# Four VectorE instructions of each weight conversion, spread over a step, in conversions that start two steps earlier

## The chip, the core and the metric

The kernel runs on one core of a Trainium2 chip. The metric is device time in microseconds (us): three runs of the kernel before gave a median of 691.45 us (688.99 to 691.76). Five engines work side by side, each through its own instructions in order: PE multiplies matrices and transposes, ACT applies functions and copies, DVE and POOL compute elementwise, and SP issues nearly all transfers from and to DRAM. Semaphores make an instruction wait for one of another engine; everything behind a waiting instruction on the same engine waits too.

## The reference

Three layers follow each other. All are computed in float32; the last layer's weights arrive as float64.

```
q_pool = mean of pairs of queries                        # 2 x 8 heads, 576 pooled queries, 1152 keys
attn   = softmax(q_pool @ k^T / 8) @ v                   # -> x: 1152 tokens x 512
e      = argmax over 8 experts of cosine(x, emb) / tau   # top-1 routing, gate = its softmax weight
y      = gate * (relu(x @ w1[e]) @ w2[e])                # w1: 512 x 1024, w2: 1024 x 512
out    = ((y @ w_a) * (y @ w_b)) @ w_out                 # w_a, w_b: 512 x 1536, w_out: 1536 x 512
```

## The kernel before

Every float32 operand is split into a rounded high part and the remainder (names ending in h or hi, and l or lo), and each product is three matmuls: high by high, high by low, low by high. ACT makes high parts, DVE or POOL subtracts to make low parts.

The program has three stages. The attention stage runs over 72 units of 128 queries. The experts' stage runs over steps m = 0 to 34; the numbers of steps below are these. The final layer runs over passes n = 1 to 37. The order of instructions on each engine is written out by hand: what stands where in the functions is what each engine gets.

The experts' stage has 32 pieces of work, one per step: a chunk of 256 of the 1024 hidden columns of one slot of tokens. Slots of two tiles (256 tokens) and of one tile (128 tokens) alternate by `ORDER`. `moe_step(m)` works on several pieces at once:

- `s1(m)` is PE's product of tokens and w1 (L890 for two tiles, 24 matmuls; L895 for one tile, 12 matmuls). `h_ev(m - 1)` takes its result one step later: for two tiles ACT makes hh (L902) and DVE hl (L903). For one tile ACT makes hs (L908), PE transposes it in `h_tr` (L915), and `h_ev2(m - 2)` one more step later makes hh on ACT and hl on DVE.
- `s2(m - 2)` is PE's product with w2 (L933; 12 matmuls for two tiles, 6 for one).
- `split1(m + 1)` makes w1h (ACT) and w1l (DVE) for the next step. `split2(m - 1)` and `split2b(m - 1)` make w2h (ACT or DVE) and two halves of w2l (POOL or DVE).
- `x_tr` and `x_ev` transpose and split the tokens of a slot: PE (L838), ACT (xhi), DVE (xlo). `y_ev` copies a finished slot out (ACT ys, L942). `load1` and `load2` issue the weights' loads on SP.

So PE's row in a step is s1(m), the transposes of hs of step m - 1, s2(m - 2), then transposes of tokens. hs(22), for example, is what PE needs between s1(23) and s2(21).

Beside that, from step 17 on, `advance` drives the conversions of the last layer's float64 weights, once at the end of every step. Each conversion covers 128 x 1024 weights; six run in the experts' stage (called conversions 1 to 6 here: w_a, w_b and w_out for the first 256 hidden columns, then the same for the next), and twelve in the final layer. `convert` is a generator; each `yield` ends its part of a step:

```
SP    raw <- DRAM          1 MB, issued in the step of W_AT; then CONV_LAG = 3 steps pass
ACT   cvt <- raw           L1075, scaled magnitude of the upper words (called Abs here)
DVE   cvt, four times      L1077, L1078, L1079, L1081 (called C1 to C4 here)
ACT   wh <- cvt            L71, high part (called W here)
POOL  wl <- cvt, wh        L75, low part in two halves
```

In the kernel before, Abs stands at the end of the third step after the load, C1 to C4 at the end of the fourth, W and the first half of wl at the end of the fifth. Loads start in steps 19, 21, 24, 27, 28, 31, so C1 to C4 stand at the ends of steps 23, 25, 28, 31, 32 and after the first elementwise work of the final layer. The tiles raw and cvt have two buffers each. In the final layer `f1` (L1165) multiplies by w_a and w_b, `f_ab` makes the product (asb, L1175; abh; abl), and `f2` (L1187) multiplies by w_out. The first products f1(0) stand in step 32, f1(1) in pass 1.

Of the kernel before, what the change touches and what calls it, by code (L numbers as in the profile page):

```python
# [14 lines left out]
U32 = mybir.dt.uint32  # L15
AF = mybir.ActivationFunctionType
ALU = mybir.AluOpType
# [26 lines left out]
LO_PARTS = range(48, 63)  # L44
ROUND1, P2_AT, DS = 3, 4, (1, 2, 1, 2, 1)
CONV_LAG, Y_LAG = 3, 4
W_AT = (19, 21, 24, 27, 28, 31)
W_AT2 = range(3, 27, 2)
W2_ACT = (1, 2, 3, 4, 5, 6, 7, 8, 9, 10, 12, 13, 16, 17, 18, 19, 21, 22, 24, 25, 27, 28, 31)
Y_AT, YB_AT = 20, 34  # L50
# [11 lines left out]
def fused(ctx, tc, q, k, v, emb, tau, w1, w2, wa, wb, wo, out):  # L62
    nc = tc.nc
# [386 lines left out]
    def pv(j, ps=None):  # L450

        pr, u = units[j]
        eT = U[j]["eT"]
        if place(j) == 0:
            G[j]["bank"] = (ps or ps_o)()
        cols = slice(0, 129) if u == 4 else slice(0, 65) if u < 4 else slice(64, 129)
        o = G[j]["bank"][:, 65 * place(j):65 * place(j) + cols.stop - cols.start]
        vh, vl = (preps[pr][x][:, :, cols] for x in ("vh", "vl"))
        for n in range(9):
            for x, v_ in ((0, vh), (0, vl), (1, vh)):  # L460
                nc.tensor.matmul(o, eT[:, 9 * x + n, :], v_[:, KEYS[n], :], start=(n == 0 and x == 0 and v_ is vh),  # L461
                                 stop=(n == 8 and x == 1))

    def xout(j):

        if not last(j):
            return
        pr, u = units[j]
        b, hp = divmod(pr, 4)
        p, w, n = G[j]["bank"], preps[pr]["ivsc"], place(j) + 1  # L470
        pg = p[:, :65 * n].rearrange("p (g d) -> p g d", g=n)
        rr = small.tile([P, 2], F32, name="r", bufs=3)
        nc.vector.tensor_scalar(out=rr[:, :n].unsqueeze(2), in0=pg[:, :, 64 * (u < 5):64 * (u < 5) + 1], scalar1=1e-9,
                                scalar2=None, op0=ALU.add)
        nc.vector.reciprocal(out=rr[:, :n], in_=rr[:, :n])
        stt = nc.vector.scalar_tensor_tensor
        if u == 4:
            for h in range(2):
                s, d = slice(64 * h, 64 * h + 64), slice(128 * hp + 64 * h, 128 * hp + 64 * h + 64)
                stt(out=xs[b][4][0:64, d], in0=p[s, 65 * h:65 * h + 64], scalar=w[s],  # L480
                    in1=rr[s, 0:1].to_broadcast([64, 64]), op0=ALU.mult, op1=ALU.mult)
        else:
            h, i = (0, u - 1) if u < 4 else (1, u - 6)
            stt(out=xt_[b][:, i:i + 2, 128 * hp + 64 * h:128 * hp + 64 * h + 64], in0=pg[:, :, h:h + 64], scalar=w,
                in1=rr.unsqueeze(2).to_broadcast([P, 2, 64]), op0=ALU.mult, op1=ALU.mult)
        G[j].clear()
        U[j].clear()
# [270 lines left out]
    def turn(kinds, columns=None):  # L758

        if cur[0] is None and queue:  # L760
            cur[:] = queue.popleft(), None
            cur[1] = next(cur[0])
        if cur[0] is not None and cur[1] in kinds:
            spare[0] = columns() if columns else None
            cur[1] = next(cur[0], None)
            if cur[1] is None:
                cur[0] = None
# [48 lines left out]
    NM = len(steps)  # L816
# [3 lines left out]
    def tiles(k):  # L820

        return 2 if k[1] < 2 else 1
# [12 lines left out]
    def x_tr(k, t, ps=None):  # L835
        pt = X[k]["pt"] = (ps or ps_t)()
        for c in range(4):
            nc.tensor.transpose(pt[:, P * c:P * c + P], X[k]["raw"][t][:, P * c:P * c + P], ident)  # L838

    def x_ev(k, t):  # L840
        pv_ = X[k].pop("pt").rearrange("p (c t) -> p c t", c=4)
        hi = X[k]["hi"][:, :, P * t:P * t + P]
        copy_hi(hi, pv_)
        sub_lo(X[k]["lo"][:, :, P * t:P * t + P], pv_, hi)
# [92 lines left out]
    def y_ev(k):  # L937
        b, s = k
        row = X[k]["row"] - (SMALL0 - 2 * NBIG * P if s >= 2 else 0)
        for t, y in enumerate(X[k].pop("y")):  # L940
            ys = moe.tile([P, DM], F32, name="ys")
            nc.scalar.activation(out=ys, in_=y, func=AF.Copy)  # L942
            nc.sync.dma_start(out=ybuf[b][row + P * t:row + P * t + P, :], in_=ys)
# [4 lines left out]
    def mt(f, m):  # L948
        if 0 <= m < NM:
            f(m)  # L950

    next_ = [1 + max(n for x in EARLY.values() for f, n in x if f == i) for i in (1, 2)]

    def moe_step(m):
        def turns(n, p=True):
            for _ in range(DS[n]):
                turn("de")
            turn("s")
            if p:
                turn("p", lambda: (ps_s().rearrange("p (j t) -> p j t", j=4), ps_s()))  # L960

        for k in X:
            if m == X[k]["l"] + 3:
                y_ev(k)
        for j in PVS.get(m - 1, ()):
            xout(j)
        turns(0, False)
        for k in X:
            if "pt" in X[k]:
                x_ev(k, X[k].pop("t"))  # L970
        mt(h_ev2, m - 2)
        mt(h_ev, m - 1)
        mt(s1, m)
        for n, j in enumerate(PVS.get(m, ())):
            pv(j, ps_m if units[j][1] == 4 else ps_o)
        turns(1)
        mt(h_tr, m - 1)
        mt(split1, m + 1)
        turns(2, False)
        mt(split2, m - 1)  # L980
        turns(3, False)
        mt(split2b, m - 1)
        mt(s2, m - 2)
        turns(4, m >= P2_AT)
        for k in X:
            t = m - X[k]["f"] + 1 + tiles(k)
            if 0 <= t < tiles(k):
                x_tr(k, t)
                X[k]["t"] = t
            if t == -1 and "raw" not in X[k]:  # L990
                x_load(k)
        la = LA[min(m, len(LA) - 1)]
        for f, x in ((load1, 0), (load2, 1)):
            while next_[x] < NM and next_[x] <= m + la[x]:
                f(next_[x])
                next_[x] += 1
# [61 lines left out]
    def convert(kind, c, dst, pool):  # L1058

        r = pool.tile([P, 1024, 2], U32, name="raw", bufs=2)  # L1060
        if kind < 2:
            src = (wa, wb)[kind].rearrange("(k p) f -> p k f", p=P)[:, :, 512 * c:512 * c + 512]
            nc.sync.dma_start(out=r.rearrange("p (k f) x -> p k (f x)", k=4), in_=src)
            sh, kw = "p (k f) -> p k f", dict(k=4)
        else:
            src = wo.rearrange("(j p) d -> p j d", p=P)[:, 2 * c:2 * c + 2, :]
            nc.sync.dma_start(out=r.rearrange("p (j d) x -> p j (d x)", j=2), in_=src)
            sh, kw = "p (j d) -> p j d", dict(j=2)
        for _ in range(CONV_LAG):
            yield  # L1070
        lo, hi = r[:, :, 0], r[:, :, 1]

        t = pool.tile([P, 1024], U32, name="cvt", bufs=2)
        tf = t.bitcast(F32)
        nc.scalar.activation(out=tf, in_=hi.bitcast(F32), func=AF.Abs, scale=2.0 ** -112)  # L1075
        yield
        nc.vector.tensor_scalar(out=tf, in0=tf, scalar1=CHI, scalar2=None, op0=ALU.min)  # L1077
        nc.vector.tensor_scalar(out=t, in0=t, scalar1=3, scalar2=1, op0=ALU.logical_shift_left, op1=ALU.bitwise_or)  # L1078
        nc.vector.scalar_tensor_tensor(out=t, in0=lo, scalar=29, in1=t, op0=ALU.logical_shift_right,  # L1079
                                       op1=ALU.bitwise_or)  # L1080
        nc.vector.scalar_tensor_tensor(out=t if dst is None else dst.bitcast(U32), in0=hi if dst is None else hi.rearrange(sh, **kw),  # L1081
                                       scalar=0x80000000, in1=t if dst is None else t.rearrange(sh, **kw),
                                       op0=ALU.bitwise_and, op1=ALU.bitwise_or)
        yield tf.rearrange(sh, **kw)

    wparts = {}
# [1 line left out]
    def weights(c, kind):  # L1088

        for f in convert(kind, c, None, wp):  # L1090
            yield
        sh = [P, 4, 256] if kind < 2 else [P, 2, DM]
        hi, lo = wparts[c, kind] = [wp.tile(sh, F32R, name=f"w{x}{kind}", bufs=2) for x in "hl"]
        copy_hi(hi, f)
        n = sh[1] // 2
        sub_lo(lo[:, :n], f[:, :n], hi[:, :n], nc.gpsimd)
        yield
        sub_lo(lo[:, n:], f[:, n:], hi[:, n:], nc.gpsimd)

    m = WP_AT  # L1100
# [104 lines left out]
    while m < NM + 3:  # L1205
# [7 lines left out]
        if m >= Y_AT:  # L1213
            drive()
        advance(m in W_AT)
        m += 1
# [37 lines left out]
    with tc.If(nc.values_load(ovf, min_val=0, max_val=2) > 0):  # L1254
        with tc.tile_pool(name="gen", bufs=1) as gen:
# [3 lines left out]
            for c in range(NC):  # L1259
                for kind in range(3):  # L1260
                    dst = wv[kind][:, :, 256 * c:256 * c + 256] if kind < 2 else wov[:, 2 * c:2 * c + 2, :]
# [5 lines left out]
            with tc.For_i(0, NE, 1) as e:  # L1267
# [8 lines left out]
                for b in range(NB):  # L1276
                    for i in range(5):
# [14 lines left out]
                        for j in range(8):  # L1292
                            nc.tensor.matmul(p, hT[:, P * j:P * j + P], w2t[:, j, :], start=j == 0, stop=j == 7)
                        nc.vector.scalar_tensor_tensor(out=yac[b][i], in0=p, scalar=gt[:, b, i:i + 1], in1=yac[b][i],
                                                       op0=ALU.mult, op1=ALU.add)
            for b in range(NB):
                for i in range(5):
# [21 lines left out]
                    m = P if i < 4 else 64  # L1319
# [5 lines left out]
CHI = 122879.9921875 * 2.0 ** -112  # L1325
# [32 lines left out]
```

## Time and profile before

| | |
|---|---|
| median of 3 runs | 691.45 us |
| the profiled execution | 693.38 us |
| its span, first to last instruction | 691.7 us |
| PE busy | 618.1 us (89%) |
| DVE busy | 493.5 us (71%) |
| ACT busy | 373.6 us (54%) |
| POOL busy | 322.3 us (47%) |
| mean granted PE clock | 0.948 of full speed |

The busy times are sums over stages of different kinds; where PE is idle is read from stretches of the span and from the waits of single instructions. An instruction of the timeline that stood idle carries in brackets for how long, and which instruction ended the wait. The experts' stage of interest (steps 22 to 34) runs from about 389 us to 462 us of the span; the final layer follows.

### The profile page before, as it was taken

To read this page: it belongs to the slowest core of one execution; us is meant where nothing else is said; L and a number is where in the kernel's file an instruction comes from. 1 tells how busy PE (TensorE), PEld (TensorE's weight loads), DVE (VectorE), ACT (ScalarE), POOL (GpSimd) and SP (SyncE) were. 2 spreads that over 40 slices of the span, in tenths; PEclk is the share of its full clock that TensorE was granted. 3 is DMA by queue.
4 is the path that set the end of the run, shared out by engine and by line. 5 is a ranking of instruction groups with operands and counts; after the bars stand their busy time and mean duration, and the time that the engine had idled before them with its cause. 6 is when DMAs were issued, how large, how long until landed. Compare 5 with 4: busy or idle time off the path is not lost.

```text
span 691.7 us, 13314 instructions
## 1 busy us (share of the span) xinstructions
PE 618.1 (89%) x5280; PEld 556.1 (80%) x5280; DVE 493.5 (71%) x796; ACT 373.6 (54%) x518; POOL 322.3 (47%) x271
## 2 busy tenths in 40 slices
PE   6688979889878788998989987969999999999996
PEld 5477767778767677998879877859999999999995
DVE  5978989887899977659947697974355575665523
ACT  3868886987665766456545675426243324233210
POOL 3958878785767941433424665673011212112100
PEclk9779999998988899999999998999999999999998
DMA  9979899998987789884898986454012213121012
GB/s 290 269 176 233 200 217 234 213 211 198 196 198 184 180 202 263 279 277 124 292 332 252 366 315 226 124 160 160 1 62 81 101 62 123 61 70 54 0 46 95
DMA packets 203075, 123.27 MB, mean 178 GB/s; under 512 B 149240, under 2 KB 174840, under 8 KB 203008
## 3 DMA queue, kind: packets, MB, share of 16 engines
q1 hardware_dynamic: 201536, 117.65, 62.3%
q0 software_dynamic: 1472, 4.72, 1.9%
q8 instruction: 43, 0.70, 0.4%
q14 instruction: 24, 0.20, 0.1%
HBM read 72.11 MB, written 13.67 MB: 124 GB/s over the span
## 4 chain that ended last, share of the span: by engine, by line
PE 49%; DVE 22%; ACT 4%; DMA 4%; issue 4%; POOL 1%; SPq 1%; DVEq 0%; ACTq 0%
PE ps_s L1165 21%; PE ps_s L890 4%; DVE nm L379 4%; PE ps_o L1187 4%; PE ps_m L1187 3%; PE ps_y L1187 3%; PE ps_o L461 2%; PE ps_s L374 2%; DVE vl L262 2%; DMA w2r<-in_moe_w_dram 2%; PE ps_m L933 2%; DMA eT<-ehl 2%; PE ps_y L933 1%; DVE cvt L1078 1%; DVE cvt L1079 1%
## 5 line engine op out<-in xcount | busy, mean ns | idle before, releaser
L407 POOL TENSOR_TENSOR ehl<-e,ehl 128x288 f16<-128x288 f32 (+1 forms) x99 | 152.3, 1557 | 63.7 <-issue 31.7
L75 POOL TENSOR_TENSOR wl<-cvt,wh 128x512 fp32r<-128x512 f32 x36 | 48.6, 1364 | 150.1 <-ACT wh L71 146.5
L75 POOL TENSOR_TENSOR w2l<-w2r,w2h 128x512 fp32r<-128x512 f32 x42 | 66.1, 1592 | 92.4 <-ACT w2h L71 46.9
L384 ACT ACTIVATE e<-ps_s,nm 128x1152 f32<-128x1152 f32 x72 | 87.8, 1220 | 37.2 <-DVE nm L379 25.1
L379 DVE TENSOR_REDUCE nm<-ps_s 128x1 f32<-128x1152 f32 x72 | 97.2, 1350 | 12.9 <-PE ps_s L374 12.7
L374 PE MATMUL ps_s<-kTh,qT 64*128 64x512 f32 (+2 forms) x480 | 98.2, 398 | 2.3 <-issue 1.2
L461 PEld LDWEIGHTS <-eT 128*128 128x128 f16 x1863 | 74.8, 102 | 16.6 <-issue 5.6
L461 PE MATMUL ps_o<-vh,eT 128*128 128x65 f16 (+1 forms) x1224 | 78.4, 203 | 10.3 <-DMA eT<-ehl 3.1
L374 PEld LDWEIGHTS ps_s<-kTh,qT 64*128 64x128 f32 x480 | 74.2, 206 | 8.5 <-issue 2.4
L461 PE MATMUL ps_o<-vl,eT 128*128 128x65 f16 (+1 forms) x612 | 73.2, 203 | 0.0
L1175 DVE TENSOR_TENSOR asb<-ps_s,asb 128x384 f32<-128x384 f32 x36 | 20.0, 554 | 69.1 <-PE ps_s L1165 69.1
L396 ACT ACTIVATE ehl<-e 128x1152 f16<-128x1152 f32 (+1 forms) x62 | 69.1, 1114 | 0.0
L71 ACT ACTIVATE abh<-asb 128x384 fp32r<-128x384 f32 x36 | 18.9, 525 | 84.3 <-DVE asb L1175 84.3
L374 PE MATMUL ps_s<-kTl,qT 64*128 64x512 f32 (+2 forms) x240 | 47.9, 367 | 1.5 <-DVE kTl L75 1.5
L1170 ACT ACTIVATE asb<-ps_s 128x384 f32<-128x384 f32 x36 | 17.7, 492 | 57.5 <-PE ps_s L1165 57.2
L374 PEld LDWEIGHTS ps_s<-kTl,qT 64*128 64x128 f32 x240 | 44.3, 209 | 2.1 <-DVE kTl L75 2.1
L75 DVE TENSOR_TENSOR w1l<-w1r,w1h 128x1024 fp32r<-128x1024 f32 x32 | 41.0, 1280 | 4.4 <-ACT w1h L71 3.6
L890 PE MATMUL ps_s<-xhi,w1l 128*128 128x256 f32 x128 | 38.0, 297 | 4.0 <-DVE w1l L75 4.0
L890 PE MATMUL ps_s<-xhi,w1h 128*128 128x256 f32 x128 | 38.4, 300 | 0.0
L75 DVE TENSOR_TENSOR abl<-asb,abh 128x384 fp32r<-128x384 f32 x36 | 20.7, 574 | 24.5 <-ACT abh L71 24.5
L890 PE MATMUL ps_s<-xlo,w1h 128*128 128x256 f32 x128 | 37.7, 294 | 0.0
L71 ACT ACTIVATE w1h<-w1r 128x1024 fp32r<-128x1024 f32 x32 | 34.0, 1063 | 0.0
(277 smaller groups left out, 1743.5 us busy)
## 6 DMA issues: line engine op xcount, KB each, us to landing
w1r<-in_moe_w_dram SPq DMA_DIRECT2D x32, 512.0 KB, 5.6
w2r<-in_moe_w_dram SPq DMA_DIRECT2D x32, 512.0 KB, 5.9
raw<-in_moe_w_a_dram SPq DMA_DIRECT2D x6, 1024.0 KB, 5.4
raw<-in_moe_w_b_dram SPq DMA_DIRECT2D x6, 1024.0 KB, 6.2
raw<-in_moe_w_out_dram SPq DMA_DIRECT2D x6, 1024.0 KB, 5.1
vs<-in_v_dram SPq DMA_DIRECT2D x8, 576.0 KB, 5.1
qs<-in_q_dram SPq DMA_DIRECT2D x16, 256.0 KB, 4.2
ks<-in_k_dram SPq DMA_DIRECT2D x7, 576.0 KB, 5.9
```

Of the source, the lines that this page charges most:

```text
L71: nc.scalar.activation(out=dst, in_=src, func=AF.Copy)
L75: (engine or nc.vector).tensor_tensor(out=dst, in0=src, in1=hi.bitcast(F32), op=ALU.subtract)
L374: nc.tensor.matmul(ps[:, c:c + n], qT[x][r:r + 64, o:o + 128], kT[y][r:r + 64, h, k0:k0 + n], start=i == 0, stop=i == len(ops) - 1)
L379: nc.vector.tensor_reduce(out=nm, in_=U[j]["ps"][:, 256:1408], axis=AX.X, op=ALU.max, negate=True)
L384: nc.scalar.activation(out=e, in_=U[j]["ps"][:, 256:1408], func=AF.Exp, bias=U[j]["nm"])
L396: nc.scalar.activation(out=ehl[:, 0, :c], in_=U[j]["e"][:, :c], func=AF.Copy)
L407: eng.tensor_tensor(out=ehl[:, 1, a:a + n], in0=U[j]["e"][:, a:a + n], in1=ehl[:, 0, a:a + n], op=ALU.subtract)
L461: nc.tensor.matmul(o, eT[:, 9 * x + n, :], v_[:, KEYS[n], :], start=(n == 0 and x == 0 and v_ is vh), stop=(n == 8 and x == 1))
L890: nc.tensor.matmul(p[:, 256 * j:256 * j + 256], a[:, kk, P * j:P * j + P], x[:, kk, :], start=(kk == 0 and x is xhi and a is w1h), stop=(k ...
L933: nc.tensor.matmul(y, a[:, j, P * t:P * t + P], w[:, j, :], start=(c == 0 and j == 0 and a is hh and w is w2h), stop=(c == 3 and j == 1 an ...
L1165: nc.tensor.matmul(p[:, :384], w[:, kk, :], y[:, kk, :], start=(kk == 0 and x == 0), stop=(kk == 3 and x == 2))
L1187: nc.tensor.matmul(F[n]["o"][t], a[:, P * t:P * t + P], w, start=(j == 0 and x == 0), stop=(j == 1 and x == 2))
```

## The change

The four DVE instructions of conversions 1 to 6 are no longer issued together. They go into a queue (`pieces`), and `moe_step` takes one from it at each of four places: ahead of s1, behind split1, behind split2 and behind split2b. A fifth entry marks the conversion as done. W_AT starts the loads earlier: steps 17, 19, 22, 24, 27, 29 in place of 19, 21, 24, 27, 28, 31, which is two steps for most, three for the fourth and one for the fifth. C1 to C4 of the six now stand in steps 22, 24, 27, 29, 32 and 34, one step later after their own load than before; W stands, as before, at the end of the fifth step after the load, which is now the step of C1 to C4 itself. The conversions of the final layer are as before.

```diff
-W_AT = (19, 21, 24, 27, 28, 31)
+W_AT = (17, 19, 22, 24, 27, 29)
...
+    pieces = deque()
+
+    def piece(n=1):
+        for _ in range(n):
+            if pieces:
+                pieces.popleft()()
+        if len(pieces) % 5 == 1:
+            pieces.popleft()()
+
     def moe_step(m):
...
         mt(h_ev, m - 1)
+        piece()
         mt(s1, m)
...
         mt(split1, m + 1)
+        piece()
         turns(2, False)
         mt(split2, m - 1)
+        piece()
         turns(3, False)
         mt(split2b, m - 1)
+        piece()
         mt(s2, m - 2)
...
         nc.scalar.activation(out=tf, in_=hi.bitcast(F32), func=AF.Abs, scale=2.0 ** -112)
         yield
-        nc.vector.tensor_scalar(out=tf, in0=tf, scalar1=CHI, scalar2=None, op0=ALU.min)
...
+        ops = (
+            lambda: nc.vector.tensor_scalar(out=tf, in0=tf, scalar1=CHI, scalar2=None, op0=ALU.min),
...
+            lambda: done.append(True))
+        if dst is None and m < NM + 3:
+            pieces.extend(ops)
+            while not done:
+                yield
+        else:
+            for f in ops:
+                f()
         yield tf.rearrange(sh, **kw)
...
         for f in convert(kind, c, None, wp):
-            yield
+            if f is None or m >= NM + 3:
+                yield
```

DVE's row around steps 22 and 23, before: xlo, hl(20), hl(21) and w1l(23) of step 22, then xlo and w1l(24) of step 23, and conversion 1 behind them.

```order
L75 TENSOR_TENSOR xlo_5995<-ps_t,xhi_5994 128x4x128
L75 TENSOR_TENSOR hl<-ps_t,hh 128x2x128
L903 SCALAR_TENSOR_TENSOR hl<-ps_s,hh 128x512
L75 TENSOR_TENSOR w1l<-w1r,w1h 128x1024
L75 TENSOR_TENSOR xlo_5995<-ps_t,xhi_5994 128x4x128
L75 TENSOR_TENSOR w1l<-w1r,w1h 128x1024
L1077 TENSOR_SCALAR cvt<-cvt 128x1024
L1078 TENSOR_SCALAR cvt<-cvt 128x1024
L1079 SCALAR_TENSOR_TENSOR cvt<-raw,cvt 128x1024
L1081 SCALAR_TENSOR_TENSOR cvt<-raw,cvt 128x1024
L75 TENSOR_TENSOR hl<-ps_t,hh 128x2x128
```

The same place of DVE's row now; L1093 to L1097 are C1 to C4.

```order
L75 TENSOR_TENSOR xlo_5997<-ps_t,xhi_5996 128x4x128
L75 TENSOR_TENSOR hl<-ps_t,hh 128x2x128
L903 SCALAR_TENSOR_TENSOR hl<-ps_s,hh 128x512
L1093 TENSOR_SCALAR cvt<-cvt 128x1024
L75 TENSOR_TENSOR w1l<-w1r,w1h 128x1024
L1094 TENSOR_SCALAR cvt<-cvt 128x1024
L1096 SCALAR_TENSOR_TENSOR cvt<-raw,cvt 128x1024
L1097 SCALAR_TENSOR_TENSOR cvt<-raw,cvt 128x1024
L75 TENSOR_TENSOR xlo_5997<-ps_t,xhi_5996 128x4x128
L75 TENSOR_TENSOR w1l<-w1r,w1h 128x1024
L75 TENSOR_TENSOR hl<-ps_t,hh 128x2x128
```

C1 stands ahead of w1l(23), and the other three ahead of step 23's xlo. In step 22 POOL has both halves of w2l, so C2, C3 and C4 follow each other.

ACT's row from step 22 to the start of step 24, before; cvt<-raw is Abs of conversion 1, hs is hs(22).

```order
L71 ACTIVATE w1h<-w1r 128x1024
L71 ACTIVATE w2h<-w2r 128x1024
L1075 ACTIVATE cvt<-raw 128x1024
L71 ACTIVATE xhi_5994<-ps_t 128x4x128
L908 ACTIVATE hs<-ps_s 128x256
L71 ACTIVATE w1h<-w1r 128x1024
L71 ACTIVATE w2h<-w2r 128x1024
L942 ACTIVATE ys<-ps_m 128x512
```

The same place of ACT's row now; wh_6145 is W of conversion 1, cvt<-raw is Abs of conversion 2.

```order
L71 ACTIVATE w1h<-w1r 128x1024
L71 ACTIVATE w2h<-w2r 128x1024
L71 ACTIVATE wh_6145<-cvt 128x1024
L1088 ACTIVATE cvt<-raw 128x1024
L71 ACTIVATE xhi_5996<-ps_t 128x4x128
L908 ACTIVATE hs<-ps_s 128x256
L71 ACTIVATE w1h<-w1r 128x1024
L71 ACTIVATE w2h<-w2r 128x1024
```

W moved from behind step 24's work to a place ahead of step 23's xhi and hs(22); it reads what C4 of the same step writes.

## Rows read from the trace of the kernel before

**Rows 1.** Busy time by stretch: engines PE, PEld, DVE, ACT, POOL, then PEclk, DMA, GB/s
```profile
396.00:408.00 12.00, 9.71 (x56) 8.78 (x55) 10.78 (x11) 8.12 (x14) 6.75 (x6) 0.86 0.95 330
408.00:420.00 12.00, 8.47 (x55) 7.43 (x53) 11.87 (x8) 7.54 (x11) 9.75 (x6) 0.93 0.66 242
420.00:446.00 26.00, 24.50 (x140) 22.12 (x141) 21.62 (x22) 11.70 (x18) 14.90 (x11) 0.90 0.65 203
446.00:480.00 34.00, 27.10 (x140) 24.29 (x139) 22.67 (x23) 17.33 (x30) 22.63 (x17) 0.95 0.50 163
```
**Rows 2.** Timeline of PE: start, duration, instruction, idle before and releaser
```profile
403.59 0.50 PE L933 MATMUL ps_o<-w2h,hl 128*128 128x512 f32 x1 [2.29 <-DVE hl L75]
419.84 0.58 PE L890 MATMUL ps_s<-xhi,w1l 128*128 128x256 f32 x1 [3.53 <-DVE w1l L75]
438.73 0.39 PE L895 MATMUL ps_s<-w1l,xhi 128*128 128x256 f32 x1 [1.50 <-DVE w1l L75]
452.87 0.51 PE L933 MATMUL ps_o<-w2h,hl 128*128 128x512 f32 x1 [1.84 <-DVE hl L75]
459.70 0.80 PE L933 MATMUL ps_o<-w2h,hl 128*128 128x512 f32 x1 [5.07 <-DVE hl L75]
```
**Rows 3.** Waits from 330 to 470: total us, times, longest
```profile
ACT wh L71 <- DVE cvt L1081: 18.5, 5, 5.5
```
**Rows 4.** The four conversion lines: ns min/median/max, first and last start
```profile
L1077 DVE TENSOR_SCALAR cvt<-cvt x18: 680/684/1777, 396.6 to 641.4; 128x1024 f32<-128x1024 f32 x18
L1078 DVE TENSOR_SCALAR cvt<-cvt x18: 693/694/3334, 397.3 to 642.1; 128x1024 uint32<-128x1024 uint32 x18
L1079 DVE SCALAR_TENSOR_TENSOR cvt<-raw,cvt x18: 1224/1226/2201, 400.7 to 642.9; 128x1024 uint32<-128x1024 uint32 x18
L1081 DVE SCALAR_TENSOR_TENSOR cvt<-raw,cvt x18: 1224/1225/2189, 402.0 to 644.1; 128x1024 uint32<-128x1024 uint32 x18
```
**Rows 5.** Timeline of DVE, step 22
```profile
391.01 0.68 DVE L903 SCALAR_TENSOR_TENSOR hl<-ps_s,hh 128x512 fp32r<-128x512 f32 x1
391.78 1.23 DVE L75 TENSOR_TENSOR w1l<-w1r,w1h 128x1024 fp32r<-128x1024 f32 x1
```
**Rows 6.** Timeline of POOL, step 22
```profile
392.78 2.65 POOL L75 TENSOR_TENSOR w2l<-w2r,w2h 128x512 fp32r<-128x512 f32 x2 [2.67 <-PE ps_t L838]
```
**Rows 7.** Timeline of ACT, end of step 22 and step 23
```profile
391.63 1.07 ACT L71 ACTIVATE w2h<-w2r 128x1024 fp32r<-128x1024 f32 x1
392.58 1.16 ACT L1075 ACTIVATE cvt<-raw 128x1024 f32<-128x1024 f32 x1
393.61 0.61 ACT L71 ACTIVATE xhi<-ps_t 128x512 fp32r<-128x512 f32 x1
394.09 0.41 ACT L908 ACTIVATE hs<-ps_s 128x256 f32<-128x256 f32 x1
```
**Rows 8.** Timeline of PE, step 23: transposes of hs, then the first of s2(21)
```profile
394.55 0.44 PE L915 MATMUL ps_t<-ident,hs 128*128 128x128 f32 x2
394.74 0.48 PE L933 MATMUL ps_m<-w2h,hh 128*128 128x512 f32 x1
```
**Rows 9.** Timeline of SP's queue, step 23
```profile
395.93 0.41 SPq L832 DMA_DIRECT2D xr<-xbuf  x1
```
**Rows 10.** Chain of waits: PE's stages without a stall (start, length)
```profile
374.44 2.88 PE ps_s L890 x24
380.30 1.43 PE ps_s L895 x12
381.73 1.39 PE ps_o L933 x6
468.51 4.19 PE ps_s L1165 x24
```
**Rows 11.** Timeline of ACT, step 24: hh(22) after the end of s2(21)
```profile
398.27 0.38 ACT L71 ACTIVATE hh<-ps_t 128x256 fp32r<-128x256 f32 x1
```

More of the change, by code (lines that the diff above doesn't have):

```diff
@@ L1076, in convert @@
         yield
-        nc.vector.tensor_scalar(out=tf, in0=tf, scalar1=CHI, scalar2=None, op0=ALU.min)
[L1078 to L1083, printed above, removed]
+        done = []
+        stt = nc.vector.scalar_tensor_tensor
+        ops = (
+            lambda: nc.vector.tensor_scalar(out=tf, in0=tf, scalar1=CHI, scalar2=None, op0=ALU.min),
+            lambda: nc.vector.tensor_scalar(out=t, in0=t, scalar1=3, scalar2=1, op0=ALU.logical_shift_left,
+                                            op1=ALU.bitwise_or),
+            lambda: stt(out=t, in0=lo, scalar=29, in1=t, op0=ALU.logical_shift_right, op1=ALU.bitwise_or),
+            lambda: stt(out=t if dst is None else dst.bitcast(U32), in0=hi if dst is None else hi.rearrange(sh, **kw),
+                        scalar=0x80000000, in1=t if dst is None else t.rearrange(sh, **kw),
+                        op0=ALU.bitwise_and, op1=ALU.bitwise_or),
+            lambda: done.append(True))
[6 more added lines that the diff above has]
+                f()
         yield tf.rearrange(sh, **kw)
```

## The prediction

> **What bounds the kernel now.** I read the busy time by stretch first, then PE's timeline, then the waits. The reader is to see that PE is the bound in the experts' stage, but not from 396 us on: its busy time falls short of the four stretches' length by 2.29, 3.53, 1.50 and 6.90 us, 14.2 us in all [rows 1]. Five waits make up all of it, and each ends with a DVE instruction, hl or w1l [rows 2]. DVE is busy 67 of these 84 us and POOL 54 [rows 1]. So DVE is late there, and the conversions make it late. In the same stretches the granted clock is 0.86, 0.93, 0.90 and 0.95: taking (1 - clock) x length as lost, 1.7 + 0.8 + 2.6 + 1.7 = 6.8 us. What the change can win is therefore 14.2 + 6.8 = 21.0 us. The same waits have another side: ACT's W stood idle for C4 18.5 us in five conversions [rows 3], while the rest of ACT's row waited behind it.
>
> **The change part by part.** Nothing is removed or added in the work: 6 loads, 6 Abs, 24 DVE instructions, 6 W and 12 halves of wl stand elsewhere. Alone, C1 to C4 take 0.68 + 0.69 + 1.22 + 1.22 = 3.8 us; beside POOL each takes about 1 us longer (1777, 2201 and 2189 ns against 684, 1226 and 1225) [rows 4]. Sum over DVE's row: the same load per conversion, only from step 22 instead of step 23 on.
>
> What does change is the distance from C4 to W. Before, C4 had a step's time until ACT came to W. Now W ends the step in which C1 to C4 stand between DVE's other work, and all of ACT's next step stands behind it. ACT comes to W as soon as w2h is made; DVE then still has w1l, C2, often a w2h or w2l, C3 and C4 ahead. So ACT must wait in every conversion, and hs or hh of the next step comes late. PE needs those.
>
> Conversion 1, on the rows of step 22. hl(21) ends at 391.69 [rows 5]. C1 runs to 392.4, w1l(23) (1.23 us) to 393.65, in place of 393.01. POOL wants its two halves of w2l from 392.78 on [rows 6], so C2 and C3 each wait for one of them: C2 ends at 393.65 + 0.98 + 0.69 = 395.35 (with gaps), C3 at 397.6, C4 at 398.85. The 0.98 is 2201 less 1226 ns [rows 4]. ACT is done with w2h(21) at 392.7 and waits 6.2 us. Then W takes 0.95 (as w2h, also 1024 columns), Abs 1.03, xhi 0.48 from start to start, and hs(22) 0.41 us [rows 7]: hs(22) ends at 401.8, where before it ended at 394.5. PE's transposes of hs(22), which stood at 394.55 with s2(21) at 394.74 behind them [rows 8], come at 401.9: 7.3 us late, 0.6 of it already from w1l(23) in s1(23). Nothing else stands in PE's row to fill it. With a lost clock of 2 us (1.7 us followed the 2.29 us wait, more the 3.53 us one [rows 1, 2]) conversion 1 costs 9.3 us. If POOL never got in the way, C4 would end 2 us sooner: 6.9 us, the lower bound; 10.2 with both POOL halves ahead of DVE.
>
> The Trainium skill, "SBUF — State Buffer" (Who interferes with whom), says that a DVE instruction in a two-port mode or with two SBUF inputs and a POOL instruction block each other for a whole instruction. The rows show 0.98 us per DVE instruction, less than POOL's 1.3 us. By the page conversion 1 would come 0.7 us later and the sum be 699.2 us.
>
> The others, by the same chain, from an event that both sides have. PE's lengths are 2.87 us for s1 and s2 of two tiles, 1.43 and 1.39 for one, 4.19 for f1 [rows 10], 0.2 for a pair of transposes [rows 8].
>
> - Conversion 2 (step 24), from the end of s2(21) on. hh(22) ended 0.9 us after it before (398.65 [rows 11]), hl(22) then takes to 1.35; C1, w1l(25), C2, w2h(23), C3, a POOL instruction and C4 end at 8.3; W, xhi and hh(23) at 10.2. PE, after s1(24), s2(22), s1(25) and transposes, wants hh(23) at 7.8: 2.4 us, then 0.3 for hl(23) and 1.0 for w1l(26). With 1.0 of clock 4.7 us; 3 to 6.
> - Conversion 3 (step 27), from the end of s1(26). C1 starts 3.7 us later, behind w1l(27), w2l(25) and yT0lo. C4 ends at 10.6, hh(26) behind W and Abs at 13.1; PE wants it at 11.1. 2.0 us, 1.0 for w1l(29), clock 0.8: 3.8 us; 2 to 5.5.
> - Conversion 4 (step 29), from the end of s1(29). C4 ends between 4 (POOL never in the way) and 6.5, hh(28) 1.4 later, w1l(31) 2.7 after that; PE wants hh(28) at 4.5. 4.0 us; 1.5 to 6.
> - Conversion 5 (step 32), from the end of s2(29). hl(30) ends at 1.35, C4 at 5.3 alone and 7.3 with two POOL instructions, hh(31) behind W and Abs at 9.8. PE wants it at 5.75, after f1(0) and s2(30): 4.3 us with hl(31), clock 1.5: 5.8 us; 3.5 to 7.5.
> - Conversion 6 (step 34) now stands ahead of the first asb. f1(1) covers it: 0.5 us for f2(0); 0 to 2.
>
> Costed at nothing: Abs ahead of hs(20) (ACT sits idle around it). The first load, 1 MB two steps earlier: the loads beside it are needed over a step later; without that cover 3.2 us (1.05 MB at the 330 GB/s of [rows 1]). The third to sixth loads now wait on SP for C4 of a conversion (raw has two buffers); behind the third stands the load of tokens that SP issued at 395.93 [rows 9], 3 us later by C4 at 398.9, and its transposes come in step 24, over 10 us later. Uncovered it would cost these 3 us. A gain is excluded for both: no wait of [rows 2] ends with a transfer.
>
> The sum: 9.3 + 4.7 + 3.8 + 4.0 + 5.8 + 0.5 = 28.1 us of waiting and clock in place of 21.0: 7.1 us more. The profiled execution took 693.38 us (span 691.7 and 1.7 around it), so it would take 700.5; the median of the runs is 1.93 us below it, so 698.5 us. The low ends make 16.9 us (4.1 less than before), the high ones 37.2 (16.2 more): 687.4 to 707.7.
>
> **Rivals.**
> - Faster: the low ends hold everywhere. The mechanism is the one resource that DVE and POOL share: conversions spread over more steps meet POOL less often, C1 to C4 take their 3.8 us, and ACT's wait at W ends within a step's slack. For it: the long C's are few enough that the median of every line is the time alone [rows 4]; they come where DVE and POOL both run behind. Against: in step 22, with nothing late yet, POOL has its w2l just when C2 to C4 come [rows 6], and W waits for C4 in any case. It decides at C4 within some 2 us of ACT's reaching W. 687 us; 0.12.
> - No difference: waits of hs and hh take the place of hl and w1l at about the same total, 21 to 24 us, conversions 2 to 5 nearer their low ends. 693 us; 0.22.
> - A queue on SP: the load that waits for C4 holds back the weights of later steps, and PE's s1 waits for w1h. 3 us more, 701.5 us. Against: a step's w1 is loaded four steps ahead, and SP would be held for only these 3 us. 0.05.
>
> **How the numbers follow.** Forecast 698.5 us, 0.61; the other cases as above. From noise alone 0.5% (3.5 us) can be told from no change. Slower: the forecast and SP's queue, 0.66. Same 0.22, faster 0.12. For eight in ten I leave out the lower end of the fast case and the upper end of the sum: 688 to 705 us.
>
> **What would show it.** Right: in step 22 ACT's W stands idle some 6 us for C4; PE's transposes of hs(22) stand idle over 4 us, released by ACT's hs; waits of W for C4 add up to over 25 us; PE's waits in L933 come from hh or hl behind W; the granted clock dips behind 402 us. hl no longer waits behind four C's except in steps 32 and 33. Wrong: PE's row from 390 to 415 us without a wait over 3 us, or ACT's W released within 2 us in step 22. Then DVE reached C4 in time, and the time falls below 691 us.

## The result and the profile after

The changed kernel took 699.17 us (median of 11 runs, 693.85 to 707.61) against 690.68 us for the kernel before (11 runs in the same session, 686.89 to 694.85): a ratio of 1.011, with a 95% interval from 1.0078 to 1.0141, which leaves out disturbed runs. It is slower by 1.1%. The profiled execution took 700.62 us with a span of 698.9 us, 7.2 us more than before.

The waits of the changed kernel from 330 to 480 us come first (engine, tile and line, what ended the wait: us in total, times, longest).

```profile
ACT wh L71 <- DVE cvt L1097: 30.6, 6, 6.7
PE ps_o L933 <- ACT hh L71: 7.9, 3, 3.8
PE ps_t L915 <- ACT hs L908: 6.8, 2, 6.4
PE ps_s L895 <- DVE w1l L75: 1.0, 3, 0.6
```

W's wait for C4 has grown from 18.5 to 30.6 us [rows 3]. The hl and w1l behind DVE's long group of four are nearly gone from PE's waits [rows 2]; what PE waits for now is hs and hh, which stand behind W on ACT.

How one becomes the other is seen in step 22. DVE's timeline (start, duration, instruction):

```profile
391.52 0.68 DVE L903 SCALAR_TENSOR_TENSOR hl<-ps_s,hh 128x512 fp32r<-128x512 f32 x1
392.12 0.68 DVE L1093 TENSOR_SCALAR cvt<-cvt 128x1024 f32<-128x1024 f32 x1
392.72 1.22 DVE L75 TENSOR_TENSOR w1l<-w1r,w1h 128x1024 fp32r<-128x1024 f32 x1
393.86 1.78 DVE L1094 TENSOR_SCALAR cvt<-cvt 128x1024 uint32<-128x1024 uint32 x1
395.67 2.17 DVE L1096 SCALAR_TENSOR_TENSOR cvt<-raw,cvt 128x1024 uint32<-128x1024 uint32 x1
397.87 1.23 DVE L1097 SCALAR_TENSOR_TENSOR cvt<-raw,cvt 128x1024 uint32<-128x1024 uint32 x1
```

C4 ends at 399.10. ACT's timeline from there (idle time before and its releaser in brackets):

```profile
392.13 1.08 ACT L71 ACTIVATE w2h<-w2r 128x1024 fp32r<-128x1024 f32 x1
399.12 1.06 ACT L71 ACTIVATE wh<-cvt 128x1024 fp32r<-128x1024 f32 x1 [5.91 <-DVE cvt L1097]
400.09 1.10 ACT L1088 ACTIVATE cvt<-raw 128x1024 f32<-128x1024 f32 x1
401.10 0.57 ACT L71 ACTIVATE xhi<-ps_t 128x512 fp32r<-128x512 f32 x1
401.57 0.37 ACT L908 ACTIVATE hs<-ps_s 128x256 f32<-128x256 f32 x1
```

ACT has nothing it may do for 5.91 us, since W is the next in its row. Then W, Abs and xhi run back to back, and hs(22) is done at 401.9. PE's timeline, all its stalls from 384 to 480 us with 0.25 us or more idle before them:

```profile
393.99 0.39 PE L895 MATMUL ps_s<-w1l,xhi 128*128 128x256 f32 x1 [0.58 <-DVE w1l L75]
402.00 0.69 PE L915 MATMUL ps_t<-ident,hs 128*128 128x128 f32 x2 [6.44 <-ACT hs L908]
416.44 0.50 PE L933 MATMUL ps_o<-w2h,hh 128*128 128x512 f32 x1 [2.09 <-ACT hh L71]
433.06 1.11 PE L1155 MATMUL ps_t<-ident,yg 128*128 128x128 f32 x4 [3.28 <-DVE yT0lo L75]
448.51 0.50 PE L933 MATMUL ps_o<-w2h,hh 128*128 128x512 f32 x1 [1.98 <-ACT hh L71]
451.20 0.58 PE L895 MATMUL ps_s<-w1l,xhi 128*128 128x256 f32 x1 [0.26 <-DVE w1l L75]
466.03 0.50 PE L933 MATMUL ps_o<-w2h,hh 128*128 128x512 f32 x1 [3.80 <-ACT hh L71]
```

Conversions 1, 2, 4 and 5 each hold PE at hs or hh; conversion 3 holds it in another way, told below. The four stretches of [rows 1] in the changed kernel (engines PE, PEld, DVE, ACT, POOL with busy us, then granted clock, DMA share, GB/s):

```profile
396.00:408.00 12.00, 6.00 (x28) 5.19 (x29) 5.46 (x6) 6.70 (x11) 7.68 (x6) 0.72 0.83 256
408.00:420.00 12.00, 9.71 (x67) 8.34 (x66) 9.15 (x10) 6.74 (x10) 6.83 (x4) 1.00 0.68 210
420.00:446.00 26.00, 22.72 (x129) 20.27 (x129) 21.91 (x21) 13.58 (x20) 17.06 (x11) 0.87 0.65 215
446.00:480.00 34.00, 27.87 (x133) 24.31 (x132) 20.41 (x21) 13.20 (x21) 21.38 (x16) 0.90 0.47 156
```

PE is idle 6.00 + 2.29 + 3.28 + 6.13 = 17.7 us there and another 1.0 between 384 and 396: 18.7 us, against 14.4 before from 384 to 478 (the 14.2 of [rows 1] and 0.2). What the clock took has to be read finer, because the clock also falls while PE is idle, and that costs nothing. The same view, cut where the clock changes:

```profile
398.30:402.00 3.70, 0.00 (x1) 0.01 (x1) 1.09 (x2) 2.88 (x5) 1.65 (x2) 0.50 0.90 272
402.00:405.00 3.00, 3.00 (x8) 2.47 (x9) 1.62 (x2) 1.83 (x2) 1.09 (x1) 0.50 0.87 346
405.00:432.20 27.20, 22.48 (x143) 19.43 (x141) 20.13 (x21) 14.80 (x23) 17.05 (x12) 1.00 0.78 242
432.20:439.00 6.80, 5.94 (x22) 5.46 (x23) 4.45 (x7) 6.45 (x9) 4.37 (x4) 0.51 0.67 211
449.00:452.80 3.80, 3.54 (x14) 2.80 (x13) 3.51 (x5) 2.21 (x3) 1.47 (x2) 0.55 0.74 300
466.00:469.80 3.80, 3.77 (x11) 3.22 (x12) 3.72 (x4) 0.60 (x1) 2.55 (x3) 0.56 0.14 22
```

Four stretches lie at or near 0.50, the lower of the two levels (1.2 GHz); the last two windows take in some 0.4 us at full speed. PE's busy time in each times (1 - clock) is 1.5 + 2.9 + 1.6 + 1.7 = 7.7 us, 7.8 in windows of half a microsecond. The kernel before has three such stretches:

```profile
404.50:408.00 3.50, 3.50 (x18) 3.41 (x17) 2.39 (x5) 3.16 (x6) 2.65 (x3) 0.52 0.71 238
418.20:425.00 6.80, 5.16 (x25) 5.16 (x25) 6.22 (x7) 3.70 (x5) 2.81 (x2) 0.51 0.47 152
459.20:463.00 3.80, 3.30 (x10) 2.92 (x11) 0.91 (x3) 2.20 (x3) 2.36 (x3) 0.55 0.01 3
```

They cost 1.7 + 2.5 + 1.5 = 5.7 us, 5.8 in half microseconds. So the account of idle time and clock is 14.4 + 5.8 = 20.2 us before and 18.7 + 7.8 = 26.5 us after, 6.3 us more. That is nearly the whole 7.2 us by which the span grew; the first matmul of f2(0) comes 7.0 us later (473.30 against 466.26).

### The profile page after: what moved, and what is told of

It is laid out like the page before. It is cut to its first block, busy times and chain, and to the rows that moved or that the text cites. A ratio compares the mean times of both kernels' runs of the same rounds, so it can differ in the third digit from the quotient of the medians.

```text
span 698.9 us, 13309 instructions
## 1 busy us (share of the span) xinstructions
PE 622.7 (89%) x5280; PEld 558.9 (80%) x5280; DVE 484.3 (69%) x796; ACT 373.2 (53%) x518; POOL 322.1 (46%) x271
## 5 line engine op out<-in xcount | busy, mean ns | idle before, releaser
L1195 ACT ACTIVATE asb<-ps_s 128x384 f32<-128x384 f32 x36 | 17.7, 491 | 56.9 <-PE ps_s L1190 56.7
L71 ACT ACTIVATE wh<-cvt 128x1024 fp32r<-128x1024 f32 x18 | 18.9, 1048 | 30.6 <-DVE cvt L1097 30.6
```

The lines of the kernel that those rows point to most:

```text
L71: nc.scalar.activation(out=dst, in_=src, func=AF.Copy)
```

## The experiments

The theory: W in the step of its own C4 blocks ACT, and with it hs and hh. Rivals: the earlier start of the loads (traffic, SP's queue) costs the time, or the spreading of C1 to C4 over DVE's row does. Kernels e1 to e4 ran on one chip, e5 to e8 on another; each ratio is to runs of the kernel before made beside it.

**e1, W one step later.** All of the change stays, except that W and wl come a step after C4:

```diff
-            if f is None or m >= NM + 3:
-                yield
+            yield
```

> The changed kernel with one edit: W (ACT's wh <- cvt) and the halves of wl behind it stand one step later, as far behind C4 as in the kernel before. Loads, Abs and the places of C1 to C4 stay as changed. Theory (ACT's row is blocked by a W that stands in the step of its own C4): ACT's waits at W fall from 30.6 us to under 8, PE's wait at the transposes of hs(22) (6.4 us) is gone, and the time is 680 to 689 us, below the kernel before. Rival (C1 to C4 between DVE's other work make hl and w1l late, wherever W stands): 696 us or more. Rival (the earlier loads, or SP held by them): 696 us or more.

Measured: 688.68 us (12 runs), ratio 0.9939 (0.991 to 0.9968), within the range given. One `yield` turns 1.1% slower into 0.6% faster. W's waits fall to a fifth, and the longest PE wait that ends with hs or hh is 0.5 us (waits from 330 to 480 us):

```profile
ACT wh L71 <- DVE cvt L1097: 6.1, 3, 3.6
PE ps_t L1154 <- DVE yT0lo L75: 3.7, 1, 3.7
PE ps_o L933 <- DVE hl L75: 2.9, 1, 2.9
PE ps_t L915 <- ACT hs L908: 0.5, 1, 0.5
```

That is the theory's strongest evidence. It speaks against both rivals too: the loads and the places of C1 to C4 are those of the changed kernel, and so is what SP has to wait for. PE's waits are 10.0 us here and the clock's share, read as above, 7.8: 17.8 us, 2.4 less than before.

**e2, the earlier starts alone.** The kernel before with the changed list, C1 to C4 together:

```diff
-W_AT = (19, 21, 24, 27, 28, 31)
+W_AT = (17, 19, 22, 24, 27, 29)
```

> The kernel before with the new starting steps alone (17, 19, 22, 24, 27, 29): C1 to C4 together at the end of a step, W one step behind them. Theory (W's place costs the time; the earlier start itself is harmless or helps): 683 to 692 us, ACT's waits at W below the 18.5 us of before. Rival (the earlier loads and Abs, or what they hold up on SP, cost the time): 696 us or more.

Measured: 692.25 us, ratio 0.9996 (0.9962 to 1.003), 0.25 us above the range given and far from the rival's. An earlier start by itself is worth nothing that can be measured, in either direction. My expectation that W would wait less than 18.5 us missed: it is 19.5 us, and PE still waits for w1l behind the four.

```profile
ACT wh L71 <- DVE cvt L1081: 19.5, 5, 5.9
PE ps_s L890 <- DVE w1l L75: 4.1, 2, 3.6
```

**e3, W in C4's step without spreading.** e2 with C1 to C4 together and W directly behind them in the same step:

```diff
         for f in convert(kind, c, None, wp):
-            yield
+            if f is None or m >= NM + 3:
+                yield
```

> As the run with the new starting steps alone, but W stands right behind C1 to C4 in the same step; the four DVE instructions stay together at the end of a step. Theory: the block of ACT is there without any spreading, since W waits for a C4 of its own step: ACT's waits at W over 20 us, 5 us or more above the run with the new starting steps alone, 692 to 702 us. Rival (the four places of the pieces cost the time): no more than 2 us from the run with the new starting steps alone.

Measured: 705.13 us (6 runs), ratio 1.0194 (1.0152 to 1.0236). That is 3 us above the range that I gave, so the loss was forecast too small. The distance from C4 to W costs 2.0% without any spreading:

```profile
ACT wh L71 <- DVE cvt L1081: 42.0, 6, 8.8
PE ps_t L915 <- ACT hs L908: 13.6, 5, 4.1
```

**e4, the spreading with the old starts.** The changed kernel with W_AT = (19, 21, 24, 27, 28, 31).

> The changed kernel with the starting steps of before (19, 21, 24, 27, 28, 31): spread pieces, W in the step of C4. Theory: slower than the kernel before like the changed one or more, 698 to 708 us, since three of the six conversions now end in the last three steps and the first of the final layer. Rival (the earlier start costs the time): 688 to 694 us, as the kernel before.

Measured: 696.79 us, ratio 1.0071 (1.0037 to 1.0105), a little under the range that I gave. W waits 28.6 us here. It is slower than before without the earlier starts, so they are not the cause. The 0.4% between this and the changed kernel is within the two intervals.

**e7, together and W a step later.** e1 with its four places replaced by one, behind split2b:

```diff
         mt(split2b, m - 1)
-        piece()
+        piece(4)
```

(the other three `piece()` of a step are taken out).

> The run with W one step later, but C1 to C4 stand together behind split2b, at the last of the four places, in the same steps. Theory (the distance from C4 to W decides, the four places hardly matter): within 3 us of the run with W one step later, 686 to 692 us. Rival (spreading them is worth something of its own): 694 us or more.

Measured: 692.36 us, ratio 1.0002 (0.9965 to 1.0038). The time lies between the two that I gave, 692 and 694 us, and the kernel before took 3 us less on this chip than on e1's; so the ratios decide, and by them it was wrong that the four places hardly matter. Against e1's 0.9939 the spreading is worth 0.6% (the difference is 0.0063, and 0.0047 either way if the two intervals, taken on two chips, are independent). The ratios make a table:

| ratio to before, starts two steps earlier | W in C4's step | W a step or more later |
|---|---|---|
| C1 to C4 together | 1.0194 (e3) | 0.9996 (e2), 1.0002 (e7) |
| C1 to C4 at four places | 1.011 (the change) | 0.9939 (e1) |

Read down, spreading gains 0.6 to 0.8%. Read across, W's place costs 1.7 to 2.0%. The change did both.

**e6, the last of the four further back.** e1's largest wait was for yT0lo, which stands behind C4 on DVE. So the last `piece()` was moved from behind split2b to behind `drive()`, which issues yT0lo.

> The run with W one step later, and C4 behind the end of a step's yT0lo in place of ahead of it. In the changed kernel PE stood 3.28 us at the transposes of y in step 27, and 3.67 us with W one step later, for a yT0lo that stands behind C3 and C4. Theory: that wait shrinks to under 2 us and the time falls by 1 to 3 us, to 685 to 688 us. Rival: the wait moves on to hl(26) or w1l(29) and the time stays at 688 to 691 us.

Measured: 689.46 us, ratio 0.9963 (0.9923 to 1.0002), not to be told from e1, nor from the kernel before. The time is the rival's. The wait for yT0lo went from 3.7 to 1.5 us, and another appeared, though neither of the two that I had named: PE's timeline shows hl(28) late in step 30, where it had not been in e1.

```profile
425.98 0.66 PE L1153 MATMUL ps_t<-ident,yg 128*128 128x128 f32 x4 [1.50 <-DVE yT0lo L75]
440.86 0.50 PE L933 MATMUL ps_o<-w2h,hl 128*128 128x512 f32 x1 [3.24 <-DVE hl L75]
```

Where DVE is behind, moving one of its instructions moves the wait.

**e5, more even distances: a miss.** e1 with Abs two steps after the load instead of three, and other starts:

```diff
-W_AT = (17, 19, 22, 24, 27, 29)
+W_AT = (17, 19, 21, 25, 27, 29)
...
-        for _ in range(CONV_LAG):
+        for _ in range(CONV_LAG if m >= NM + 3 else 2):
```

> The run with W one step later, Abs one step sooner behind its load (two steps pass in place of three), and starts at 17, 19, 21, 25, 27, 29, so that C1 to C4 stand in steps 21, 23, 25, 29, 31 and 33: none in steps 26 to 28, which carry yT0lo, and the first in a step in which PE has 5.9 us of its own work in place of 2.9 in step 22. If DVE's and POOL's load per step decides what is left: 682 to 687 us. If the three conversions in steps 21 to 25 crowd each other: 688 to 693 us.

Measured: 697.06 us, ratio 1.0083 (1.0045 to 1.012); neither number was right. The same fault came back through another instruction (ACT's timeline, then PE's):

```profile
406.91 1.12 ACT L1088 ACTIVATE cvt<-raw 128x1024 f32<-128x1024 f32 x1 [8.60 <-POOL wl L75]
457.04 1.13 ACT L1088 ACTIVATE cvt<-raw 128x1024 f32<-128x1024 f32 x1 [11.77 <-POOL wl L75]
```

```profile
409.60 0.69 PE L915 MATMUL ps_t<-ident,hs 128*128 128x128 f32 x2 [6.62 <-ACT hs L908]
459.74 0.69 PE L915 MATMUL ps_t<-ident,hs 128*128 128x128 f32 x2 [5.01 <-ACT hs L908]
```

cvt has two buffers. Abs of a conversion may begin when POOL has made wl of the one before the last. Where those two start four steps apart (17 and 21, 25 and 29), Abs stands at the end of the very step whose end also has the second half of that wl. For conversion 3 that half is here, in POOL's timeline, and Abs starts when it ends, at 406.9:

```profile
404.64 2.24 POOL L75 TENSOR_TENSOR wl<-cvt,wh 128x512 fp32r<-128x512 f32 x1
```

Abs stands in ACT's row as W does, and the hs behind it is late in the same way.

**e8, e5 with starts that leave room.** The same two steps to Abs, and W_AT = (17, 19, 22, 25, 27, 30): any two conversions that share a buffer of cvt start five or six steps apart (six for 19 and 25, five for the other three pairs), so Abs comes at least one step behind that half of wl.

> The run with C1 to C4 in steps 21, 23, 25, 29, 31 and 33 lost 8.6 and 11.8 us of ACT's time at Abs of conversions 3 and 6: Abs writes the cvt tile that POOL's wl of two conversions before still reads (two buffers), and hs stood behind it on ACT, as it stood behind W in the changed kernel. Those two pairs of starts are 4 steps apart, the others 6. Here the starts are 17, 19, 22, 25, 27, 30, every second one 5 or 6 apart (6 for the second and third pair). Theory (an ACT instruction whose producer is late blocks hs and hh, whichever it is): both waits at Abs fall under 2 us, PE's 6.6 and 5.0 us at the transposes of hs are gone, and the time is 683 to 689 us at a before of 690. Rival (the load on DVE and POOL in steps 21 to 25 was the cause): 693 us or more.

Measured: 687.63 us (12 runs), ratio 0.9925 (0.9885 to 0.9964), faster than both kernels. From 375 to 480 us Abs and W still wait, longer than the 2 us each that I expected, but in pieces that PE mostly doesn't feel:

```profile
ACT wh L71 <- DVE cvt L1097: 8.2, 4, 3.4
ACT cvt L1088 <- POOL wl L75: 4.9, 2, 3.5
```

PE's waits are 10.8 us and the clock's share 3.2. Against e5 (19.7 and 4.4) only two starts differ, each by a step. That moves C1 to C4 of conversions 3 and 6 by a step as well, so the time alone does not rule out the load on DVE and POOL; the waits do, since the 8.6 and 11.8 us at Abs and the 6.6 and 5.0 us of PE behind them are gone. With two steps to Abs it also waits for its own load, 12.6 us in e5 and 7.9 in e8, where e1 has no such wait. Against e1 the time cannot be told apart.

One account was made for every kernel: waits of PE plus clock, from 384 us to 11.7 us behind the first matmul of f2(0), where before has 20.2 us. It is 31.5 in e3, 26.5 in the change, 24.0 in e5, 23.4 in e4, 19.6 in e2, 18.0 in e7, 17.8 in e1, 14.5 in e6 and 14.0 in e8. The order is that of the ratios but for e6 against e1 and e7 against e2 and before, which their intervals don't part. The sizes follow only roughly: e3's span is 15.8 us longer than that of before, its account 11.3. Each is one execution, and they differ already where the conversions begin: s1(21) starts at 382.96 us in before, and between 380.69 (e1) and 387.07 (e7) in the others. The account also puts e7 next to e1, so where the 0.6% of the spreading comes from is not shown.

## Why the prediction came out right, point by point

The time predicted was 698.5 us, the time measured 699.17. Against the kernel before, 7.1 us more were predicted; the medians are 8.5 us apart, the profiled spans 7.2. The mechanism was the one named, and two of its terms were off in opposite directions.

- **W behind its own C4.** Shown by e1 against the change, and by e3 against e2. Conversion 1, worked out on rows, came out closely. hl(21) ended 0.51 us later in this execution than in the rows of before (392.20 against 391.69); with that taken off, C2, C3 and C4 ended at 395.1, 397.3 and 398.6, where 395.35, 397.6 and 398.85 had been worked out. W waited 5.91 us for 6.2, PE 0.58 + 6.44 = 7.0 us for 7.3. The low end of 6.9 us is not the sum's own: 9.3 less 2 us is 7.3.
- **The clock terms.** I took (1 - clock) x length as lost, which counts time in which PE was idle anyway: 6.8 us before, really 5.8. For conversion 1 I put 2 us; it was 1.5. The clock fell at 398.2, while PE stood idle, and came back at 405.0, so only 3 us of work ran at half speed.
- **Conversion 2** was oversized: 4.7 us predicted (3 to 6), 2.09 + 0.15 = 2.2 measured, below its range. The wait for hh(23) was there (2.4 predicted), but w1l(26) came almost in time and the clock stayed at 1.00.
- **Conversion 3** was undersized and took another path: 3.8 predicted (2 to 5.5) at hh(26) and w1l(29), 3.28 + 2.9 of clock = 6.2 measured, above its range. PE stopped earlier, at the transposes of y (L1155), because the buffer they write is freed by yT0lo, which stands behind C4 on DVE:

```profile
430.23 2.17 DVE L1097 SCALAR_TENSOR_TENSOR cvt<-raw,cvt 128x1024 uint32<-128x1024 uint32 x1
432.33 0.68 DVE L75 TENSOR_TENSOR yT0lo<-ps_t,yT0hi 128x512 fp32r<-128x512 f32 x1
```

  That chain does not go through W, and e1 keeps it (3.7 us). The forecast counted the yT0lo ahead of C1 and left out this one behind C4. With the old starts neither the kernel before nor e4 has such a wait; e2 and e7, which don't spread, have 1.7 and 2.6 us. So it comes with the earlier start of conversion 3.
- **Conversions 4, 5 and 6**: 4.0, 5.8 and 0.5 predicted. Measured 1.98 + 0.26 + 1.6 = 3.8, 3.80 + 1.7 = 5.5, and 0.1 of other waits. W of conversion 6 waited 1.79 us, covered by PE's work as assumed.
- **The sum**: 28.1 - 21.0 = 7.1 us predicted; 26.5 - 20.2 = 6.3 us by the finer account. Part of the closeness is luck, since conversions 2 and 3 cancel.
- **What was costed at nothing.** The earlier loads and the third to sixth loads waiting on SP: from 384 to 480 us no wait of PE over 0.1 us ends with a transfer. e2 shows no cost of the earlier loads. There the third load comes a step behind C4 of conversion 1, so SP's wait for C4 is tested by e1, which has it as the changed kernel does and is faster than before. The rival of SP's queue is out.
- **The faster rival** said that spread conversions meet POOL less often. In step 22 C2 and C3 took 1.78 and 2.17 us, both held up by POOL as the forecast had it. But that spreading itself gains was true: e1 against e2 and e7, and the change against e3, put it at 0.6 to 0.8%. That it gains by meeting POOL less often is not shown. I had only the loss in view, and did not say that the same change with W one step later would win.
- **The Trainium skill**, "SBUF — State Buffer" (Who interferes with whom), has whichever of DVE and POOL issues first hold the shared ports for its whole instruction, while the other is blocked. The forecast took 0.98 us per meeting from [rows 4] and saw less than a whole instruction in it. It passed over the longest row there, a C2 of 3334 ns, of conversion 1 before the change. That C2 stood behind both of POOL's halves of w2l, 2.64 us more than its 0.69 alone for their 2.55 us (DVE's row, then POOL's):

```profile
397.34 3.33 DVE L1078 TENSOR_SCALAR cvt<-cvt 128x1024 uint32<-128x1024 uint32 x1
397.56 2.55 POOL L75 TENSOR_TENSOR w2l<-w2r,w2h 128x512 fp32r<-128x512 f32 x2
```

  In step 22 of the changed kernel C2 took 1.78 us against 0.69 alone and C3 2.17 against 1.23, 1.1 and 0.95 us more. POOL's halves of w2l had begun there some 0.6 us ahead of each, at 393.29 and 395.04, and the pair took longer too:

```profile
393.29 3.46 POOL L75 TENSOR_TENSOR w2l<-w2r,w2h 128x512 fp32r<-128x512 f32 x2 [2.30 <-ACT w2h L71]
```

  So these rows agree with the page: what a DVE instruction loses is the rest of POOL's instruction, and it is less than the whole only where POOL had begun earlier. The 0.7 us worked out by the page did not come, since POOL was under way each time; C4's end came 0.25 us sooner than worked out.

## What to carry to other kernels

An instruction put into an in-order row needs distance from what it waits for, counted in the work of the engine that makes it: ask which instructions stand behind it on its own engine and who waits for those, not only whether the engine is idle. A change that spreads a producer's work over a step delays its last piece, so the consumer must move with it; here one `yield` was worth 1.7%. The reuse of a buffer is the same kind of wait (e5), so the distance between two users of a buffer belongs in the same calculation.

## What was not expected of the hardware

- The granted clock sometimes fell only after a PE wait had ended: to half speed from 449.4 us after one of 1.98 us that ended at 448.5, and from 404.6 us before the change after one of 2.29 us that ended at 403.6 [rows 2]. It did not fall after one of 2.09 us (416.44 us, with 1.00 until 432.2). A wait of about 2 us cost 1.6 or 1.7 us more, or nothing; what decides that was not settled.
- A long wait can cost less clock than a short one: after 6.44 us of waiting 1.5 us was lost, after 3.28 us 2.9, because in the first most of the low stretch lay in PE's idle time.
